# VectorE sums the last rows, and the last attention segment runs without memory work: a two-layer kernel with recurrent-memory attention and a gated MLP

## The chip, the cores and the metric

The kernel runs on one core of one Trainium2 chip. The metric is the device time of one execution in microseconds; for the kernel before, the median of three runs is 1624.42 (1624.3 to 1626.09). One execution was also taken with the hardware profiler; all durations below are from that one.

The core's engines run side by side, each through its own list of instructions: TensorE (PE; its weight loads are PEld), VectorE (DVE), ScalarE (ACT), GpSimd (POOL) and SyncE (SP). SP and POOL issue the DMA transfers. PSUM, into which TensorE writes, has eight banks, numbered 0 to 7 here.

## The reference

```python
h = concatenate([mem, xs])                  # 8 memory rows and the 32 tokens of segment s
q, k, v = h @ Wq, h @ Wk, h @ Wv            # 32 heads of 128
p = softmax(mask(q @ k.T * scale))          # memory seen by all, tokens causal
o = (p @ v) @ Wo
mem = o[:8]; outs.append(o[8:])             # the next segment starts from this memory
...
z = gelu(x @ w_in)                          # gMLP: 512 -> 1376
z2 = layernorm(z[:, 688:])
g = w_sp @ z2 + b_sp                        # 2048 x 2048, over the tokens
return (z[:, :688] * g) @ w_out
...
x = x + A(layernorm(x)); x = x + B(layernorm(x))    # twice, with the same weights
```

`x` is 2048 tokens of 512 values. The attention A goes through 64 segments one after the other, because each needs the memory rows that the one before produced.

## The kernel before, in words

The program is two times `a_block` (attention) and `b_block` (gMLP). In both, the instructions of TensorE, VectorE and ScalarE stay in the order in which the Python code writes them (`ORDERED`, `manual_schedule`); those of POOL and SP are placed by a planner, which may issue a load well ahead of its place in the text, as soon as its buffer is free.

**A segment** (`segment`, L912). For segment s TensorE projects 32 rows (the memory of s and its tokens) in pieces: Q and K of one half of the heads into the tile psQ, then psm, psK, psV (`mm_chunk`, L721). VectorE turns these 128x512 pieces (`qk_T`, L932). Scores psS, their exponentials on ScalarE, and the masked E (`close`, L967) follow. `pv` multiplies by the values into psO; `sums_ahead` and `sums_memory` give the softmax denominators of the memory rows, `sums_tokens` those of the token rows (psT). ScalarE forms the reciprocals as exp(-ln) (Rm for the memory rows, Rt for the token rows, L1089 and L1092). `memory_out` (L1026) writes the memory rows of uT, which the output projection `wo_pairs` (px, L798) and `wo_rest` (L805) need at once: they produce the memory of the next segment, which VectorE folds (`fold`, L894 and L896) and puts into hT (`build_hA`, L903 and L904). The next segment's psQ starts when hT is there. The token rows are written by `tok_out` (L1029) and `last_out` (L1032) later, and their output projection is done one segment later beside the next memory rows; rows that this scheme leaves out (the last eight of each segment, from the oB tiles) are projected in groups of 16 segments by `y_part` into the tile pwB, and summed over four parts in yB (L834, L840). `store_o` (L909, L910) and `store_last` (L811) write the attention's output o_d to HBM.

`fill` puts independent matmuls into a segment: `y_part`'s or, for a later 128-token block, the projections of its last rows (`b_units`). `HALVED` holds one base-36 digit for each segment: how many groups of four 512-column matmuls are issued as two times four of 256 columns.

**Row work between the blocks.** gMLP needs x plus the attention's output, and its layer norm. `y_load` (L222, L224, on POOL) loads 128 rows of x into y_x and of o_d into y_o; the sum is made in halves by VectorE (`y_half`, L238) or, for the last four groups of rows (8 to 11), whole by POOL (`y_add`, L228); `y_stats` makes the statistics in three pieces (two halves L150, one aggregate L152); `y_norm` (L249) writes the normalised rows into ln_xn (two buffers) and stores them to xb_d. Rows are numbered in groups of 128: NB = 16 of them, so NB - 8 to NB - 5 are rows 8 to 11, which the loop's last four segments (s = 60 to 63) work on. Three hooks, `spare1`, `spare2` and `spare3`, place such pieces inside a segment, and `tail` and `loads` at its end. `x_stats` makes the same statistics of the input rows two blocks ahead.

**The end of `a_block`.** After the last segment the remaining statistics and norms of rows 10 and 11 are made, then TensorE runs the closing pass: 64 matmuls into pw (L1245) that project the last segment's tokens. ScalarE copies pw to o_end (L1248) and VectorE adds its halves (L1251). Then `b_block` begins: `project` (L296) makes z for 16 tiles, each into a PSUM tile pz of three banks.

**PSUM banks** in this kernel: accA and accB are banks 0 and 1 (changed round in the second block), att 2 and 3, attO0 4 and 5, attO1 6 and 7. The first pz and every second one take banks 2, 3 and 4, the others 5, 6 and 7. Before, pw lies in accB.

Of the kernel before, what the change touches and what calls it, by code (L numbers as in the profile page):

```python
# [29 lines left out]
LATE_STATS = 14  # L30
HALVED = (
    "0090030030800300605070749020807690007088900050807390307085901070",
    "5080030080200400307790006080729040807490207086900070708190507080",
# [629 lines left out]
def a_block(tc, c, rows, front, MV_in, RS_in, MV_out, RS_out, ahead, wo, S, first):  # L663
# [6 lines left out]
    with ExitStack() as ctx:  # L670
# [137 lines left out]
        yB, stores = {}, []  # L808
# [4 lines left out]
        def wo_last(parts, pwB):  # L813

            for k, units in enumerate(parts):
                for t, (src, h) in enumerate(units):
                    nc.tensor.matmul(pwB[32 * t:32 * t + 32, :], lhsT=src[:, h, :], rhs=wo.head(h).rearrange("p (kt g el) -> p g kt el", kt=4, g=4),  # L817
                                     start=(k == 0), stop=(k == 7), tile_position=(0, 32 * t))
                yield

        def y_part(G, q, last=False):

            groups = [oBs[G][:, :, 32 * g:32 * g + 32] for g in range(4)]
            if last:
                parts = [[(groups[g], 8 * q + k) for g in range(3)] + [(groups[q], 24 + k)] for k in range(8)]
            else:
                parts = [[(groups[g], 8 * q + k) for g in range(4)] for k in range(8)]
            pwB = accA.tile([P, DM], F32, name="pwB")
            for k, _ in enumerate(wo_last(parts, pwB)):
                if k in (0, 3):  # L830
                    yield

            def add(lo, n, src):
                nc.vector.tensor_tensor(out=yB[G][lo:lo + n, :], in0=pwB[src:src + n, :], in1=yB[G][lo:lo + n, :], op=ALU.add)  # L834

            def out():
                n = 96 if last else P
                if q == 0:
                    yB[G] = wk.tile([P, DM], F32, name="yB", bufs=1)
                    nc.vector.tensor_copy(yB[G][0:n, :], pwB[0:n, :])  # L840
                else:
                    add(0, n, 0)
                if last:
                    if q == 2:
                        store_last(G, 0, 64, nc.sync)
                    add(32 * q, 32, 96)
                    if q == 2:
                        store_last(G, 64, 96, nc.sync)
                elif q == 3 and G < NB // 4 - 2:
                    stores.append(lambda: store_last(G, 0, P, nc.sync))  # L850
                elif q == 3:
                    store_last(G, 0, P, nc.sync)

            adds.append(out)
            yield

# [55 lines left out]
        def segment(s, fill, spare1, spare2, spare3, tail, loads):  # L912
# [150 lines left out]
            close(1)  # L1063

# [3 lines left out]
            sums = (psO[1][:, 0, 384:512].rearrange("p (g n) -> p g n", g=2), psO[1][:, :, 320:384])  # L1068
            if not (first and s == 0):
                fill()  # L1070
            sums_ahead(sums[0])
# [3 lines left out]
            memory_out(0, sums[0])  # L1075
            spare1(E)
            pv(1)
            sums_memory(1, sums[1])
            sums_tokens(psT)
            memory_out(1, sums[1])  # L1080
# [7 lines left out]
            Rt = segp.tile([P, 2, 512], F32, name="Rt", tag="Rt", bufs=1)  # L1088
            nc.scalar.activation(out=Rt[:], in_=psT[:], func=ACT.Ln)  # L1089
            for r in range(2):  # L1090
                rt = Rt[:, :, 256 * r:256 * r + 256]
                nc.scalar.activation(out=rt, in_=rt, func=ACT.Exp, scale=-1.0)  # L1092
            run(turns)
            spare2()
# [7 lines left out]
            tok_out(0)  # L1102
            last_out(0)
            fill()
            run(copies)
            tok_out(1)
            last_out(1)
# [23 lines left out]
        seen = pers.tile([P, 1], BF16, name="seen")  # L1131

        def y_load(y, o):
            rows.y_load(y, first, nc.gpsimd, rows.pool.tile([P, DM], F32, name="y_x")[:], o)()
# [8 lines left out]
        for s in range(NSEG):  # L1143
# [12 lines left out]
            def spare1(E):  # L1156
                for y, added in ys:
                    if added:
                        y_stats(y, 0)
                    elif tb < NB - 1:  # L1160
                        if j4 < 3:
                            rows.y_half(y, first, 0, nc.gpsimd)
                    else:
                        nc.gpsimd.tensor_copy(seen[:], E[:, 1, 0, 0:1])
                        rows.y_add(y, first, nc.gpsimd, nc.gpsimd)
                if s == NSEG - 1:
                    y_load(NB - 5, rows.pool.tile([P, DM], F32, name="y_o")[:])
                    rows.y_add(NB - 5, first, nc.gpsimd, nc.gpsimd)
# [4 lines left out]
                if (first or tb + 2 >= LATE_STATS) and j4 == 1 and tb + 2 < NB:  # L1173
                    x_stats(tb + 2, 0)
# [6 lines left out]
            def spare2():  # L1181
                if first and s == 8:
                    c["cast_bsp"] = c["load_bsp"]()
                if first and s == 12:
                    c["cast_bsp"]()
                for y, added in ys:
                    if added:
                        y_stats(y, 1)
                    elif tb < NB - 1:
                        rows.y_half(y, first, int(j4 < 3), nc.gpsimd)  # L1190
                if (first or tb + 2 >= LATE_STATS) and j4 == 1 and tb + 2 < NB:
                    x_stats(tb + 2, 1)

            def spare3():
                for y, added in ys:
                    if added:
                        y_stats(y, 2)
                    elif tb < NB - 1 and j4 == 3:
                        rows.y_half(y, first, 1, nc.gpsimd)
                if (first or tb + 2 >= LATE_STATS) and j4 == 1 and tb + 2 < NB:  # L1200
                    x_stats(tb + 2, 2)
                if s == NSEG - 1:
                    for k in range(3):
                        y_stats(NB - 6, k)

            def tail():
                if j4 == 1 + 2 * (first and tb == 0) and tb + 1 < NB:
                    spread_v(blk_state[tb + 1])
                if tb == NB - 1:
                    if j4 != 2:  # L1210
                        front.load_w(j4)
                    if j4 > 0:
                        front.load_rows(j4 - 1)
                if ys and ys[0][1]:
# [6 lines left out]
            def loads():  # L1221
                if due and s < NSEG - 1 and (not ys or tb == NB - 1):
                    y = due.pop(0)
                    ys.append([y, False])
                    if tb < NB - 1 or j4 == 0:
                        y_load(y, rows.pool.tile([P, DM], F32, name="y_o")[:])
                    elif j4 == 1:
                        nc.vector.memset(rowsB[:, 0, 0:1], 0.0)
                        y_load(y, rowsB[:].rearrange("p a n -> p (a n)").bitcast(F32))
                    else:  # L1230
                        y_load(y, wo.VX[0][:].rearrange("p j r e -> p (j r e)").bitcast(F32))

            segment(s, lambda n=1: [next(more, None) for _ in range(n)], spare1, spare2, spare3, tail, loads)
        assert due == [NB - 5] and ys == [[NB - 6, True]]
# [6 lines left out]
        pw = accB.tile([P, 512], F32, name="pw")  # L1241
        for i in range(H // 2):
            for k in range(4):
                h = 2 * i + k % 2
                nc.tensor.matmul(pw[32 * k:32 * k + 32, :], lhsT=ends[k // 2][:, h, :], rhs=wo.head(h).rearrange("p (kt g el) -> p g kt el", kt=4, g=4),  # L1245
                                 start=(i == 0), stop=(i == H // 2 - 1), tile_position=(0, 32 * k))
# [46 lines left out]
```

## Time and profile before

| what | value |
|---|---|
| median of the runs (lowest, highest) | 1624.42 us (1624.3, 1626.09) |
| the profiled execution: its time, its span | 1624.41 us, 1622.7 us |
| mean granted TensorE clock | 0.996 |
| TensorE, VectorE, ScalarE, GpSimd busy | 97%, 75%, 65%, 18% |
| one undisturbed segment | 10.00 us |
| s = 61, 62 in the first block, 125, 126 in the second | 10.01, 10.48, 10.00, 10.48 us |

The profile gives for each group of instructions its line, engine, operation and tiles, the busy time, the mean duration of one, and how long the engine stood idle just before them with the instruction that ended it. A wait is written as `engine line <- releaser`, with its sum, its number and its longest. A timeline gives the start and the duration of each instruction in order. Segment 61 of the first block begins at 659.55 us, 62 at 669.56 and 63 at 680.04; in the second block, the segments are counted on, so that 64 is its first: 125 begins at 1448.80, 126 at 1458.80 and 127 at 1469.28.

### The profile page before, as it was taken

What the parts mean: (1) busy time and instruction counts of PE and PEld (TensorE: products, weight loads), DVE (VectorE), ACT (ScalarE), POOL (GpSimd) and SP (SyncE); (2) the same over time, 40 slices, a digit from 0 to 9 for tenths busy, and PEclk for the clock granted to TensorE, in tenths of its full rate; (3) what the DMA queues carried; (4) which work ended last, traced back from release to release, by engine and by line L of the source; (5) the groups of instructions that cost most, each with busy time, mean ns of one, the idle gap of its engine ahead of it and who ended that gap; (6) DMA issues with size and microseconds to landing.
All of it is one profiled execution on the core that took longest, in us unless ns stands there. A gap on an engine that the chain in (4) does not pass through costs nothing.

```text
span 1622.7 us, 93662 instructions
## 1 busy us (share of the span) xinstructions
PE 1568.9 (97%) x42251; PEld 992.3 (61%) x42274; DVE 1212.3 (75%) x3181; ACT 1062.4 (65%) x2278; POOL 286.3 (18%) x604
## 2 busy tenths in 40 slices
PE   3899999999999999999999999999999999999999
PEld 1456666666666666666656666666666666665565
DVE  3677777788887887884467777777888788878722
ACT  2577777777777777661047777777777777775400
POOL 5111111111211122320011111111121112214000
PEclk9899999999999999999999999999999999999999
DMA  9322212213322334276962222222233233335696
GB/s 346 110 47 43 43 43 44 46 43 76 82 55 44 76 90 82 88 191 140 208 183 48 44 50 47 46 47 48 62 95 81 47 69 98 92 56 171 141 199 162
DMA packets 264760, 149.47 MB, mean 92 GB/s; under 512 B 198680, under 2 KB 240784, under 8 KB 264360
## 3 DMA queue, kind: packets, MB, share of 16 engines
q1 hardware_dynamic: 251128, 99.66, 28.6%
q0 software_dynamic: 13232, 43.82, 8.4%
q8 instruction: 331, 5.42, 1.4%
q14 instruction: 69, 0.57, 0.1%
HBM read 59.68 MB, written 37.19 MB: 60 GB/s over the span
## 4 chain that ended last, share of the span: by engine, by line
PE 92%; DMA 4%; ACT 1%; DVE 1%; issue 1%; POOL 1%; SPq 0%; POOLq 0%; DVEq 0%
PE psQ L721 13%; PE psK L721 13%; PE psb L721 9%; PE pg L396 9%; PE px L798 8%; PE psV L721 7%; PE psm L721 7%; PE psO L805 6%; PE pz L296 5%; PE psO L1007 3%; PE pwB L817 3%; PE py L439 2%; PE psT L999 2%; PE psS L955 2%; DMA Wk_sb<-in_A_Wk_dram 1%; DMA Wo_high<-in_A_Wo_dram 1%
## 5 line engine op out<-in xcount | busy, mean ns | idle before, releaser
L721 PEld LDWEIGHTS <-hT 128*32 128x32 bf16 x13904 | 365.8, 96 | 286.1 <-DVE hT L904 67.0
L932 DVE STREAM_TRANSPOSE QQ<-rows 128x512 bf16<-128x512 bf16 x256 | 179.3, 701 | 19.6 <-ACT rows L929 12.7
L932 DVE STREAM_TRANSPOSE KA<-rows 128x512 bf16<-128x512 bf16 x256 | 176.3, 689 | 12.6 <-ACT rows L929 11.3
L929 ACT CAST rows<-psQ 128x512 bf16<-128x512 f32 x256 | 142.2, 584 | 20.1 <-PE psQ L721 19.4
L396 PE MATMUL pg<-z,wspT 128*128 128x344 bf16 x1024 | 154.3, 309 | 0.0
L1026 DVE TENSOR_TENSOR uT<-psO,Rm 128x128 bf16<-128x128 f32 x256 | 74.6, 291 | 105.6 <-PE psO L1010 57.1
L1092 ACT ACTIVATE Rt<-Rt 128x512 f32<-128x512 f32 x256 | 147.3, 622 | 4.1
L1029 DVE TENSOR_TENSOR uT<-psO,Rt 128x384 bf16<-128x384 f32 x256 | 140.8, 550 | 11.6 <-ACT Rt L1092 4.5
L964 ACT ACTIVATE S<-psS 128x224 bf16<-128x224 f32 x256 | 91.4, 357 | 82.8 <-PE psS L959 82.8
L721 PE MATMUL psQ<-Wq_sb,hT 128*32 128x512 bf16 x2048 | 135.2, 381 | 8.7 <-ACT Rt L1089 5.1
L798 PEld LDWEIGHTS <-uT 128*32 128x32 bf16 x4608 | 111.0, 96 | 47.8 <-DVE uT L1026 32.5
L798 PE MATMUL px<-Wo,uT 128*32 128x256 bf16 x3840 | 134.8, 274 | 0.6 <-DMA Wo<-in_A_Wo_dram 0.6
L721 PE MATMUL psK<-Wk_sb,hT 128*32 128x256 bf16 (+1 forms) x2796 | 134.7, 322 | 0.0
L721 PE MATMUL psK<-Wv_sb,hT 128*32 128x512 bf16 (+1 forms) x2620 | 134.6, 333 | 0.0
L721 PE MATMUL psm<-Wq_sb,hT 128*32 128x512 bf16 x2048 | 134.4, 379 | 0.1
L721 PE MATMUL psQ<-Wk_sb,hT 128*32 128x512 bf16 x2048 | 134.2, 379 | 0.0
L721 PE MATMUL psV<-Wv_sb,hT 128*32 128x512 bf16 (+1 forms) x2344 | 133.6, 351 | 0.0
L1089 ACT ACTIVATE Rt<-psT 128x1024 f32<-128x1024 f32 x128 | 131.0, 1024 | 3.1
L396 PEld LDWEIGHTS <-wspT 128*128 128x128 bf16 x1024 | 100.2, 98 | 53.2
L805 PE MATMUL psO<-Wo_high,uT 128*32 128x128 bf16 x7168 | 124.3, 220 | 1.9 <-DMA Wo_high<-in_A_Wo_dram 1.9
L888 POOL COPY KX<-old 128x128 bf16<-128x128 bf16 x128 | 68.2, 547 | 305.1 <-PE psS L959 248.8
L1024 ACT ACTIVATE Rm<-psO 128x128 f32<-128x128 f32 x256 | 71.0, 277 | 74.0 <-PE psO L981 74.0
(194 smaller groups left out, 2895.0 us busy)
## 6 DMA issues: line engine op xcount, KB each, us to landing
o_d<-o_sb SPq DMA_DIRECT2D x126, 64.0 KB
vb_d<-front SPq DMA_DIRECT2D x30, 256.0 KB
VX<-vb_d SPq DMA_DIRECT2D x120, 64.0 KB
ln_x<-xd SPq DMA_DIRECT2D x26, 256.0 KB
y_o<-o_d POOLq DMA_DIRECT2D x22, 256.0 KB, 3.6
xd<-y_o POOLq DMA_DIRECT2D x22, 256.0 KB, 3.0
Wq_sb<-in_A_Wq_dram POOLq DMA_DIRECT2D x8, 512.0 KB, 10.1
Wk_sb<-in_A_Wk_dram POOLq DMA_DIRECT2D x8, 512.0 KB, 11.1
```

Of the source, the lines that this page charges most:

```text
L296: nc.tensor.matmul(pz[:, c0:c1], lhsT=xnT[:, kt, :], rhs=w_in_sb[:, kt, c0:c1], start=(kt == 0), stop=(kt == KT - 1))
L396: nc.tensor.matmul(pg[t][:, k, 0:344], lhsT=wsp[t][:, st, :], rhs=z(st, 344 * k, 344 * k + 344), start=(st == 0), stop=(st == NT - 1))
L721: mms.append(nc.tensor.matmul(ps[32 * cg:32 * cg + 32, n * k:n * k + n], lhsT=lhs(kt, cg), rhs=r[:, m * k:m * k + m], start=(kt == 0), sto ...
L798: nc.tensor.matmul(px[at:at + 32, 0:256], lhsT=lhs[:, h, :], rhs=wo_rhs(h, slice(k + 2, None, -2) if h % 2 else slice(k, None, 2)), start= ...
L805: nc.tensor.matmul(pw[32 * cg:32 * cg + 32, :], lhsT=lhs[:, h, :], rhs=wo_rhs(h, cg), start=False, stop=(h == H - 1), tile_position=(0, 32 ...
L929: return r, mms, nc.scalar.copy(r[:], ps)
L932: nc.vector.transpose(out=QQ[:, j % 2, :, 0:32] if j < 2 else KA[:, j % 2], in_=r[:])
L964: return nc.scalar.activation(out=S[:, r], in_=psS[:, r, 0:224], func=ACT.Exp, scale=scale)
L1026: nc.vector.tensor_tensor(out=hview(uT_cur[:], r, 24, 32), in0=oview(r, 0, 8), in1=rm.rearrange("p g (n q) -> p g n q", q=8), op=ALU.mult)
L1029: nc.vector.tensor_tensor(out=hview(uT_nxt[:], r, 0, 24), in0=oview(r, 8, 32), in1=rview(r, 0, 24), op=ALU.mult)
L1089: nc.scalar.activation(out=Rt[:], in_=psT[:], func=ACT.Ln)
L1092: nc.scalar.activation(out=rt, in_=rt, func=ACT.Exp, scale=-1.0)
```

## The change

Three things are changed in `a_block`, and one table.

The row work gets one more hook, `spare0`, which stands behind the second masked E (`close(1)`), ahead of `pv`. A segment's pieces of row work are spread over four hooks, as a rule one piece in each: the first half sum or first half statistic in `spare0`, the second in `spare1`, the aggregate in `spare3`. `x_stats` is spread over two segments (j4 = 1 and 2). 

The last rows, 8 to 11, are no longer summed by POOL but by VectorE, in the places that the new table `FINAL` names: its keys are (segment within the last block, hook), its entries (row minus 8, piece, index). Row 8 is summed in s = 61, row 9 in s = 62 and 63, row 10 at the end of 63; row 11 behind the loop.

In the last segment the memory rows' work is left out (nothing follows that would need a memory: the rows that it would have written are overwritten by `store_last`), the token factors are formed where it stood, and `tok_out` and `last_out` come ahead of the fold. The closing pass's tile pw is taken from att in place of accB, and its matmuls start with the upper heads. The last group's three parts of pwB are summed in PSUM in one tile, ScalarE copies the extra rows into yB, and one VectorE add and one store close it.

`HALVED` has other digits; most are larger.

```diff
+FINAL = {(1, 0): ((0, "sum", 0),), (1, 1): ((0, "sum", 1),),
+         (2, 0): ((0, "stats", 0),), (2, 1): ((0, "stats", 1),), (2, 2): ((1, "sum", 0),), (2, 3): ((0, "stats", 2),),
+         (3, 0): ((1, "sum", 1),), (3, 1): ((1, "stats", 0),), (3, 2): ((1, "stats", 1),),
+         (3, 3): ((1, "stats", 2), (2, "sum", 0), (2, "sum", 1))}
 HALVED = (
-    "0090030030800300605070749020807690007088900050807390307085901070",
-    "5080030080200400307790006080729040807490207086900070708190507080",
+    "0386908690878078906080729040708070807080708070708190507070807084",
+    "6392907690869080030807070807080709060708290407080707080708080649",
 )
...
-            pwB = accA.tile([P, DM], F32, name="pwB")
+            if not last or q == 0:
+                held["pwB"] = accA.tile([P, DM], F32, name="pwB")
+            pwB = held["pwB"]
...
+                if last:
+                    nc.scalar.copy(yB[G][32 * q:32 * q + 32, :], pwB[96:128, :])
+                    if q == 2:
+                        add(0, 96, 0)
+                        store_last(G, 0, 96, nc.sync)
+                    return
...
             close(1)
+            spare0()
...
+            ends_here = s + 1 == NSEG
...
             pv(0)
-            memory_out(0, sums[0])
+            if not ends_here:
+                memory_out(0, sums[0])
             spare1(E)
             pv(1)
...
-            memory_out(1, sums[1])
+            if ends_here:
+                spare2()
+                token_factors((1, 0))
+            else:
+                memory_out(1, sums[1])
             run(copies)
             px = accB.tile([P, 512], F32, name="px")
             wo_pairs(px, uT_cur)
...
+            if ends_here:
+                fill()
+                for r in (1, 0):
+                    tok_out(r)
+                    last_out(r)
+            else:
+                token_factors((0, 1))
+                run(turns)
+                spare2()
...
+            def final(slot):
+                for y, op, k in FINAL.get((j4, slot), ()) if tb == NB - 1 else ():
+                    (y_stats if op == "stats" else y_sum)(NB - 8 + y, k)
+
+            def spare0():
+                final(0)
                 for y, added in ys:
                     if added:
                         y_stats(y, 0)
                     else:
-                        nc.gpsimd.tensor_copy(seen[:], E[:, 1, 0, 0:1])
-                        rows.y_add(y, first, nc.gpsimd, nc.gpsimd)
+                        y_sum(y, 0)
...
+                if (first or tb + 2 >= LATE_STATS) and j4 in (1, 2) and tb + 2 < NB:
+                    x_stats(tb + 2, j4 - 1)
...
-        assert due == [NB - 5] and ys == [[NB - 6, True]]
+        assert due == [NB - 5] and not ys
+        y_norm(NB - 7, nc.sync)
+        for k in range(3):
+            y_stats(NB - 6, k)
+        for k in range(2):
+            y_sum(NB - 5, k)
         for k in range(3):
             y_stats(NB - 5, k)
         run(copies)
         for y in (NB - 6, NB - 5):
             y_norm(y, nc.sync)
         ends = (uT[NSEG % 2], oBs[NB // 4 - 1][:, :, 96:128])
-        pw = accB.tile([P, 512], F32, name="pw")
-        for i in range(H // 2):
+        pw = att.tile([P, 2, 512], F32, name="pw")[:, 0, :]
+        for n in range(H // 2):
+            i = (n + H // 4) % (H // 2)
```

## The prediction

> **What bounds the kernel now.** I read the page first (busy shares, slices, the chain), then the list of waits, then the timelines of the places that the diff touches: the segments s = 61 and s = 63 of the first attention block (from 659.55 and 680.04 us), and their twins 125 and 127 in the second (from 1448.80 and 1469.28). Times with a plus are counted from the start of a segment, which is its first psQ matmul.
>
> ```profile
> span 1622.7 us, 93662 instructions
> PE 1568.9 (97%) x42251; PEld 992.3 (61%) x42274; DVE 1212.3 (75%) x3181; ACT 1062.4 (65%) x2278; POOL 286.3 (18%) x604
> PE   3899999999999999999999999999999999999999
> PE 92%; DMA 4%; ACT 1%; DVE 1%; issue 1%; POOL 1%; SPq 0%; POOLq 0%; DVEq 0%
> PEld L721 <- DVE hT L904: 67.0, 243, 0.9
> PEld L721 <- issue: 10.4, 28, 1.2
> POOL y_o L224 <- DMA o_d<-yB: 17.6, 3, 9.2
> ```
>
> TensorE is busy 97% of the span, and a clean segment takes 10.00 us of it. So VectorE work is worth something only where TensorE stands waiting for it, and new VectorE work costs only where it makes TensorE wait. The waits for hT are mostly weight loads that come early and cost nothing. The "issue" line is TensorE out of instructions. POOL's last line is the one to remember: the load of a summed row waits for the store of yB.
>
> **Moved row work (spare0, FINAL).** VectorE runs strictly in program order, so an operand that comes late holds all that is written behind it.
> ```profile
> 662.18 0.56 SPq L811 DMA_DIRECT2D o_d<-yB  x1
> 665.66 0.54 POOL L224 DMA_DIRECT2D y_o<-o_d  x1 [9.25 <-DMA o_d<-yB]
> 665.70 0.38 DVE L967 TENSOR_TENSOR E<-S,maskN 128x448 bf16<-128x448 bf16 x1
> 666.57 0.29 DVE L1026 TENSOR_TENSOR uT<-psO,Rm 128x128 bf16<-128x128 f32 x1 [0.49 <-PE psO L1010]
> 669.08 1.16 POOL L228 TENSOR_TENSOR y_o<-y_o,y_x 128x512 f32<-128x512 f32 x1 [1.87 <-DMA y_o<-o_d]
> ```
> This is s = 61. VectorE is free from 666.08 to 666.57, and the new spare0 goes there. A half sum takes 0.41 us (L238: 13.2 us over 32), 0.34 from issue to issue, a half statistic 0.42: one piece fits into the 0.49 us if its row is there. In the ordinary segments I took each y_o landing from the transfers: it is later than the slot by enough to push uT (normally at +7.02) in six segments, 37, 53, 99, 101, 115 and 117, by 0.20, 0.07, 0.36, 0.15, 0.82 and 0.50 us (landing + 0.09 to start + 0.34 - 7.02). TensorE's output pass px waits for uT, with nothing between: +2.1 us. Before, the same sum stood behind uT.
>
> At s = 61 the late row is row 8. Its load can't be issued before the yB store has landed (665.66 = +6.11; in segment 125 at +6.81), and lands at +9.38 and +10.61. FINAL's entry (1, 0) puts its first half sum ahead of uT: uT comes at 9.38 + 0.09 + 0.37 = +9.84 instead of +7.02, and at about +11.0: +2.8 and +4.0 us, +6.8 together. Queued behind are uT, px, the fold and hT, so all of it reaches TensorE. In the profile of before the same lateness only held POOL's adds, each of 1.16 us, which nobody waited for; that these adds and POOL's `seen` copies (0.20 us) go is worth nothing, since POOL is busy 18%. Its loads and stores stay as many. SP's two yB stores at the end become one (0.7 us less on a queue that is not late). If a gap of POOL's L224 moved by 1 us, the term would be 4.8 to 8.8.
>
> **Statistics of x spread over two segments.** Three pieces in one segment push hT late: TensorE's psQ starts 0.2 to 0.3 us late in segments 36, 38, 50, 69, 104, 114 and 118, 0.6 in 54. Spread, they fit: -1.3. At s = 62 the two yB operations of the segment before (0.68 + 0.69) stand ahead of the first transposes and TensorE waits 0.48 us; ScalarE's copy takes their place: -0.48 per block, -1.0. ScalarE is 65% busy and its 0.6 us copy stands where nobody waits, so it is costed at nothing; were that cover gone, at 0.6 per block.
>
> **HALVED.** A unit of a digit turns four matmuls into eight and costs about 2 ns (a segment without takes 10.00, with nine units 10.02); the digits go from 404 to 531 in all: +0.3 us. But they also shift where TensorE's instruction pages end. All stalls of L721 for "issue" inside segments sit at instruction 194 or 195 of a page of 256, in ten places (0.2 to 1.2 us), 4.9 us in all, where a page was run in about 3.2 us. The new digits make two segments and their eight units five pages, so that ends fall at fixed places with a shortest page of 3.4 to 3.6 us: I take -2.2 (bounds -4.9, all stalls gone, and +1.5, five more of 0.3 us).
> Were the Trainium skill ("Runtime: NRT & Kernel Launch", Instruction fetch mechanics) right that the end of a 16 KiB block of 256 instructions is mostly hidden, this term would be 0 and the time 2.2 us longer; the ten stalls speak for a cost that is not hidden.
>
> **The end of the block.**
> ```profile
> 692.43 0.39 PE L1245 MATMUL pw<-Wo,uT 128*32 128x512 bf16 x2 [1.16 <-DVE uT L1029]
> 694.59 0.55 DVE L249 TENSOR_SCALAR ln_xn<-rowsB,MV,RS 128x512 bf16<-128x512 f32 x1
> 696.19 6.12 PE L296 MATMUL pz<-front 128*128 128x512 bf16 x29
> 696.51 0.57 ACT L1248 COPY o_end<-pw 128x512 f32<-128x512 f32 x1
> 698.15 0.55 DVE L249 TENSOR_SCALAR ln_xn<-y_o,MV,RS 128x512 bf16<-128x512 f32 x1 [1.68 <-DMA xb_d<-ln_xn]
> 698.73 1.40 DVE L1251 TENSOR_TENSOR o_end<-pw,o_end 32x512 f32<-32x512 f32 x2
> ```
> Before, in s = 63, TensorE waits 0.86 us for the first transposes (1.80 in segment 127), 1.16 for uT ahead of the closing pass pw (L1245), then runs pw 3.8 us and the first projection pz at +16.15 (+17.09). Without memory work and with the token factors early, pw can start at about +9.9, when the fill ends, and pz at about +13.5: -2.65 and -3.6, -6.25 in all.
>
> What is late next is pw's bank. Before, pw lay in accB's bank, which pz does not use; so its readers, ScalarE's o_end copy and VectorE's two adds, could end at 700.13, 3.9 us after pz began. Now pw takes the att tile: banks 2 and 3. The first pz takes banks 2 to 4. So TensorE waits until the copy and both adds are done, and they stand last in VectorE's order. I followed that order with the rows above: last_out(0) ends at +10.4; the fold, o_sb, the aggregate of row 9 and both sums of row 10 to +12.1; ScalarE's yB copy, then VectorE's add on 96 rows +12.6 to +13.3 (0.69); y_norm of row 9 to +13.8; statistics of row 10 to +14.6, two sums and the statistics of row 11 to +16.2; y_norm of row 10 beside; then y_norm of row 11. This takes the ln_xn buffer of row 9, whose store lands 3.0 us after its norm (694.59 + 0.55 to 698.15), so at +16.9 to +17.4; then the adds, 1.40, to +18.86. pz begins at +18.9 instead of +13.5: +5.4. In segment 127 that store took 4.2 us (1485.33 to 1489.51); between 3.0 and 4.2 I take 3.6: +6.0. Together +11.4; at least 7.0 if the norms' stores are quick (the adds then end at about +17), at most 14 if row 11 is also late by 1.3 us in each.
>
> **Clock.** The profile shows what a long idle does.
> ```profile
> 22.20:25.80 3.60, 0.02 (x4) 0.09 (x1) 0.00 (x0) 0.72 (x3) 1.12 (x3) 1.00 1.04 395
> 25.80:29.20 3.40, 3.29 (x32) 1.39 (x35) 2.26 (x5) 1.13 (x3) 1.53 (x3) 0.50 1.01 405
> 42.85:46.26 3.41, 1.47 (x42) 1.01 (x43) 2.30 (x8) 0.86 (x3) 0.88 (x3) 1.00 1.01 344
> 46.26:49.60 3.34, 0.61 (x6) 0.13 (x6) 0.00 (x0) 0.00 (x0) 0.00 (x0) 0.50 1.03 350
> ```
> After the length of the stretch stands TensorE's busy time; the last three numbers are the granted clock, the DMA share and GB/s. After 3.6 us with none the clock was 0.50 for 3.4 us, and also after 3.41 us with 1.47 busy; a full stretch at half speed costs 1.7 us. The idle of 5.4 and 6.0 us at pz: 1.7 each. That of 2.85 and 4.05 us at s = 61: 0.85 to 1.7; I take 0.8 and 1.2 with the chance that a stretch holds too much work. Sum +5.4 (bounds 0 and 6.8).
> The Trainium skill ("TensorE: Matmul & The Clock Gate", Part 1) asks for a whole idle window of 3413 ns. By that rule the 2.85 us costs nothing and the 4.05 us seldom does: about 2.0 us less than my sum, 1637.2. The row from 42.85 with 1.47 us of work in it was followed by half clock, which speaks against it.
>
> **Sum.** The profiled execution took 1624.41 (span 1622.7 and 1.7 around it), as the median of the runs, 1624.42. Gains: -1.3 - 1.0 + 0.3 - 2.2 - 6.25 = -10.4. Losses: 2.1 + 6.8 + 11.4 = 20.3. Clock 5.4. Together +15.3: 1639.7; I say 1639, since each loss is nearer to its upper end than to its lower.
>
> **The rivals.**
> A, not slower: pz does not wait for pw. If pz took its first banks elsewhere, or the adds ended by +13.5 (that decides), 11.4 and 3.4 of clock go: 1639.7 - 14.8 = 1624.9, from 1621 to 1627. For it: last_out ends almost 3 us earlier than before (692.95 + 0.28 = +13.2). Against: banks 2 to 4 are pz's in this kernel, and nothing in the diff moves o_end ahead of the norms. Chance 0.10.
> B: s = 61 does not stall. If row 8 lands by +6.5, 6.8 and 2.0 of clock go: 1630.9. Against: its load was issued at +6.11 and +6.81, and lands 3.3 to 3.8 us later; the store's place is unchanged. Chance 0.12.
> C: the change does what it says and neither wait shows: 1624.4 - 10.4 + 2.1 = 1616.1. Chance 0.08.
> D, my forecast: both waits. Chance 0.70, within it 1630 (quick stores, no half clock: -4.4 - 5.4) to 1646 (the upper bounds of the losses and the clock: +2.0 + 2.6 + 1.4).
>
> **How the numbers follow.** About 0.2% (3.25 us) is what a measurement of this kernel can tell from no change. C is faster, and 0.03 of A: 0.11. The rest of A is the same: 0.07. B and D are slower: 0.82. The range must leave out no more than 0.2: without A and C, 0.18, it runs from 1628, which takes in most of B (down to 1626.5 with quick stores), to 1646.
>
> **What would show it.** In s = 61 and 125 VectorE's half sum of row 8 waits for the y_o transfer, and uT comes near +9.8 and +11.0, with TensorE idle 2.8 and 4.0 us in front of px; the first pz matmul of each block waits 5 to 6 us for VectorE's o_end, at +18.9 and +19.5; half clock in the stretches behind; fewer and shorter stalls for issue. The prediction is wrong if pz starts by +15, if uT in s = 61 stays near +7, or if L721's stalls for issue grow.

## The result and the profile after

The changed kernel takes 1642.89 us (median of six runs, 1640.08 to 1646.95) against 1624.36 (six runs, 1622.82 to 1626.09): slower by 1.16%, with a 95% interval of the ratio of 1.0103 to 1.0129. The profiled execution took 1642.10, its span is 1640.4. The forecast was 1639 with a range of 1628 to 1646.

The lines of the page and of the list of waits that answer to those shown of before:

```profile
span 1640.4 us, 94604 instructions
PE 1571.5 (96%) x42719; PEld 1007.9 (61%) x42742; DVE 1211.5 (74%) x3183; ACT 1063.5 (65%) x2276; POOL 278.9 (17%) x590
PE   4899999999999999989999999999999999998999
PE 91%; DMA 5%; DVE 2%; ACT 2%; issue 1%; POOL 0%; DVEq 0%; POOLq 0%
PEld L725 <- DVE hT L910: 65.4, 250, 0.9
PEld L725 <- issue: 11.1, 25, 1.5
POOL y_o L228 <- DMA o_d<-yB: 17.1, 3, 9.4
```

TensorE's busy time is nearly the same, 1571.5 us against 1568.9, and the span is 17.7 longer: the loss is TensorE waiting, or working at half clock. Two of the 40 slices of TensorE's row have an 8 that had a 9, the 18th (697 to 738 us) and the 37th (1476 to 1517): these are the starts of the two gMLPs.

Here is s = 61 of the first block (it starts at 658.73 now), VectorE's, POOL's and TensorE's timelines in turn:

```profile
664.87 0.38 DVE L973 TENSOR_TENSOR E<-S,maskN 128x448 bf16<-128x448 bf16 x1
669.24 0.43 DVE L242 TENSOR_TENSOR y_o<-y_o,y_x 128x256 f32<-128x256 f32 x1 [3.98 <-DMA y_o<-o_d]
669.58 0.28 DVE L1032 TENSOR_TENSOR uT<-psO,Rm 128x128 bf16<-128x128 f32 x1
...
664.95 0.54 POOL L228 DMA_DIRECT2D y_o<-o_d  x1 [9.36 <-DMA o_d<-yB]
...
669.92 1.89 PE L802 MATMUL px<-Wo,uT 128*32 128x256 bf16 x30 [3.76 <-DVE uT L1032]
```

VectorE stands 3.98 us in front of the half sum of row 8, whose load could be issued only at 664.95; uT is behind it, and TensorE's px behind uT. The end of the block (s = 63 starts at 683.85):

```profile
697.25 0.53 DVE L253 TENSOR_SCALAR ln_xn<-rowsB,MV,RS 128x512 bf16<-128x512 f32 x1
700.97 0.58 ACT L1287 COPY o_end<-pw 128x512 f32<-128x512 f32 x1
701.77 0.55 DVE L253 TENSOR_SCALAR ln_xn<-y_o,MV,RS 128x512 bf16<-128x512 f32 x1 [0.96 <-DMA xb_d<-ln_xn]
702.34 1.40 DVE L1290 TENSOR_TENSOR o_end<-pw,o_end 32x512 f32<-32x512 f32 x2
704.00 2.29 PE L300 MATMUL pz<-front 128*128 128x512 bf16 x5 [6.69 <-DVE o_end L1290]
```

pw ended at about 697.3, and the first pz began 6.69 us later, when the two adds that read pw had ended at 703.74. In the second block it waits 7.43 us. There the profile names a store of ln_xn as what came last; the adds ended 0.58 us before pz, and the experiments on the bank below decide.

Where the 17.7 us are, from the starts of the segments in the two profiles:

| place | before | after | difference | forecast |
|---|---|---|---|---|
| to the end of segment 11 | 164.98 | 163.55 | -1.4 | 0 |
| segments 12 to 60 and 65 to 124 | 1097.04 | 1097.67 | +0.6 | -1.1 |
| segments 61 and 125 | 20.00 | 29.01 | +9.0 | +8.8 |
| segments 62 and 126 | 20.96 | 20.02 | -0.9 | -1.0 |
| segments 63 and 127, to the first pz | 33.24 | 41.05 | +7.8 | +5.2 |
| from the first pz to the end of each gMLP | 276.46 | 279.03 | +2.6 | +3.4 |

The first row holds the loading of the weights at the start; in the profiles of all the kernels here it lies between 163.55 and 167.14.

### The profile page after: what moved, and what is told of

It is laid out like the page before. It is cut to its first block, busy times and chain, and to the rows that moved or that the text cites. A ratio compares the mean times of both kernels' runs of the same rounds, so it can differ in the third digit from the quotient of the medians.

```text
span 1640.4 us, 94604 instructions
## 1 busy us (share of the span) xinstructions
PE 1571.5 (96%) x42719; PEld 1007.9 (61%) x42742; DVE 1211.5 (74%) x3183; ACT 1063.5 (65%) x2276; POOL 278.9 (17%) x590
## 4 chain that ended last, share of the span: by engine, by line
PE 91%; DMA 5%; DVE 2%; ACT 2%; issue 1%; POOL 0%; DVEq 0%; POOLq 0%
PE psQ L725 13%; PE psK L725 13%; PE psb L725 9%; PE pg L400 9%; PE px L802 8%; PE psm L725 7%; PE psV L725 6%; PE psO L809 6%; PE pz L300 5%; PE psO L1013 3%; PE pwB L821 3%; PE py L443 2%; PE psT L1005 2%; PE psS L961 1%; DMA Wk_sb<-in_A_Wk_dram 1%; DMA Wo_high<-in_A_Wo_dram 1%
## 5 line engine op out<-in xcount | busy, mean ns | idle before, releaser
L725 PEld LDWEIGHTS <-hT 128*32 128x32 bf16 x14412 | 378.7, 96 | 277.3 <-DVE hT L910 65.4
L802 PEld LDWEIGHTS <-uT 128*32 128x32 bf16 x4608 | 112.1, 97 | 54.4 <-DVE uT L1032 39.0
L725 PE MATMUL psQ<-Wq_sb,hT 128*32 128x512 bf16 x2048 | 134.1, 381 | 7.7 <-ACT Rt L1080 5.1
L725 PE MATMUL psK<-Wv_sb,hT 128*32 128x512 bf16 (+1 forms) x2852 | 134.3, 319 | 1.0 <-issue 1.0
L725 PE MATMUL psK<-Wk_sb,hT 128*32 128x256 bf16 (+1 forms) x2952 | 134.0, 314 | 0.0
L725 PE MATMUL psQ<-Wk_sb,hT 128*32 128x512 bf16 x2048 | 133.7, 379 | 0.3 <-issue 0.3
L725 PE MATMUL psm<-Wq_sb,hT 128*32 128x512 bf16 x2048 | 133.5, 379 | 0.0
L725 PE MATMUL psV<-Wv_sb,hT 128*32 128x512 bf16 (+1 forms) x2464 | 133.3, 342 | 0.0
L809 PEld LDWEIGHTS <-uT 128*32 128x32 bf16 x7168 | 115.7, 98 | 3.7 <-issue 3.1
```

Of the source, the lines that this page charges most:

```text
L725: mms.append(nc.tensor.matmul(ps[32 * cg:32 * cg + 32, n * k:n * k + n], lhsT=lhs(kt, cg), rhs=r[:, m * k:m * k + m], start=(kt == 0), sto ...
L802: nc.tensor.matmul(px[at:at + 32, 0:256], lhsT=lhs[:, h, :], rhs=wo_rhs(h, slice(k + 2, None, -2) if h % 2 else slice(k, None, 2)), start= ...
L809: nc.tensor.matmul(pw[32 * cg:32 * cg + 32, :], lhsT=lhs[:, h, :], rhs=wo_rhs(h, cg), start=False, stop=(h == H - 1), tile_position=(0, 32 ...
```

## The experiments

Each is compared with runs of the kernel before on its own chip; a "changed kernel" is the one above. The kernel before has medians of 1622.55 to 1626.74 there, so a difference of 2 us between runs that were measured at different times means little by itself, and the ratios count. Each kernel has one profile, of one execution.

**Each wait alone.** First the sums of row 8, put where a late row holds nothing that the segment needs:

```diff
-FINAL = {(1, 0): ((0, "sum", 0),), (1, 1): ((0, "sum", 1),),
+FINAL = {(1, 3): ((0, "sum", 0), (0, "sum", 1)),
```

> The changed kernel with one edit: both half sums of row 8 stand in the last hook of s = 61 (behind hT), not ahead of uT. Theory (two separate waits): the stall in s = 61 and 125 with its half clock goes, 5.1 + 3.9 us by the changed kernel's segments, so 1642.9 - 9.0 = 1634; VectorE then reaches the first transposes of s = 62 up to 0.75 us later, which may give back 0.2 per block. Rival 1 (VectorE's row work as a whole is too much, wherever it stands): the time stays above 1640. Rival 2 (the stall is only moved: the late row holds VectorE in the later hook just as long): s = 62 gets longer by 2 us or more and the time is 1638 to 1641.

Measured: 1634.09 us (before 1623.78; ratio 1.0063, 1.0048 to 1.0078). VectorE in s = 61, and the two segments 61 and 125 as stretches (length, TensorE busy, and so on):

```profile
667.22 0.25 DVE L910 STREAM_TRANSPOSE hT<-memT 128x64 bf16<-128x64 bf16 x1
667.57 0.74 DVE L242 TENSOR_TENSOR y_o<-y_o,y_x 128x256 f32<-128x256 f32 x2
```
```profile
657.21:667.21 10.00, 10.00 (x310) 6.00 (x309) 8.00 (x22) 7.09 (x16) 2.19 (x5) 1.00 0.31 88
1450.82:1460.83 10.01, 10.01 (x332) 6.65 (x332) 8.01 (x22) 7.08 (x16) 2.17 (x5) 1.00 0.32 90
```

The same two operations behind hT cost nothing: TensorE is busy in 10.00 of 10.00 us, and s = 62 stays at 10.02. The stall is the place of the sum in VectorE's order, not the work. Both rivals fall.

Then the bank. pw goes back to accB; px lies there before it, so its readers come earlier, and the exponentials of the token factors go behind ScalarE's copy of px (the first call makes the logarithm alone):

```diff
-                token_factors((1, 0))
+                token_factors(())
...
+                token_factors((1, 0), False)
                 fill()
+                fold(px, cross, t1, beside)
                 for r in (1, 0):
                     tok_out(r)
                     last_out(r)
...
-        pw = att.tile([P, 2, 512], F32, name="pw")[:, 0, :]
+        pw = accB.tile([P, 512], F32, name="pw")
```

> The changed kernel with the closing pass's tile back in accB's bank; so that accB is free in time, the fold of the last segment is made before the last rows of uT (ScalarE's copy beside it ahead of the two exponentials). Theory (the first pz waits for the readers of pw because they share bank 2): pz begins at +13.5 to +14.2 in place of +20.15 and +20.90, and the half clock behind it goes (1.0 to 1.9 each): 1642.9 - 6.4 - 7.1 - 3 = 1626.4. Rival (pz is late for another reason, its rows or weights, or VectorE's backlog holds the first tiles anyway): pz still begins at +17 or later and the time is above 1636.

Measured: 1634.43 us (ratio 1.0075, 1.0049 to 1.0101). The wait was there because of the bank: pz now begins at +13.61 and +13.62, while the adds still end at +19.50 and +21.17. But only 8.5 of the 16.5 us came back. In the second block, from the first pz to the end took 143.04 us, against 137.91 in the changed kernel and 136.33 before. TensorE's waits among the pz matmuls of the second block, from its timeline:

```profile
1495.47 4.81 PE L300 MATMUL pz<-front 128*128 128x512 bf16 x24 [1.20 <-ACT z L301]
1507.65 9.47 PE L300 MATMUL pz<-front 128*128 128x512 bf16 x48 [2.72 <-DMA front<-xb_d]
1523.92 9.47 PE L300 MATMUL pz<-front 128*128 128x512 bf16 x48 [2.16 <-DMA front<-xb_d]
```

A tile has 12 of these matmuls. The third tile waits for the GELU of the first, which stands behind the factor of row 11, the copy of pw and a table load on ScalarE; the seventh and the thirteenth wait for their rows, which come back transposed from xb_d. None of this showed before, when pz began at +16.15 and +17.09: the profile has no wait among its pz matmuls. A start at +13.6 runs into what was ready only later.

**Both edits.**

> Both edits together. Theory: the two waits are independent and add: 1642.9 - 9.0 - 16.5 = 1617.4, faster than before by 7 us, since what is left are the gains of the change less the late rows. Rival (the end of the block gives part back, because the later row 8 pushes VectorE's chain behind it): 1620 to 1624.

Measured: 1626.29 us (before 1623.78; ratio 1.0011, 0.9999 to 1.0022), not 1617.4, and above the rival's range too. The two waits add, 8.8 and 7.8 us. Of the 8.9 us that are missing, 6.8 are again behind pz: 140.68 and 142.56 us to the ends of the two blocks (before 140.12 and 136.33).

```profile
1499.75 11.10 PE L300 MATMUL pz<-front 128*128 128x512 bf16 x48 [2.29 <-DMA front<-xb_d]
```

The seventh tile of the second block waits 2.29 us for its rows, and the 48 matmuls from there take 11.10 us in place of 9.47, since the granted clock is 0.50 for 3.4 us from 1499.67 on.

**The chain behind row 11.** In the run with both edits, VectorE stood 2.82 us in front of row 11's norm for ln_xn's buffer, with SP's stores and, behind them, the transposes. Here that norm has a buffer of its own:

```diff
-        for y in (NB - 6, NB - 5):
-            y_norm(y, nc.sync)
+        y_norm(NB - 6, nc.sync)
+        rows.y_norm(NB - 5, MV_out[:, NB - 5, 0:1], RS_out[:, NB - 5:NB - 4], nc.sync, rowsB[:, 0, :])
```

> Both edits (row 8 later, accB), and the norm of row 11 written to a buffer that is free, so that it does not wait 2.8 us for the store of row 9's. Theory (what held the end of the block in the run with both edits is the chain behind row 11's norm: o_end, SP's stores and then the transposes of xb_d, for which the eighth and later tiles wait 2.3 and 0.5 us in the second block): these waits go, 1626.3 - 2.8 = 1623.5. Rival (the transposes are late because transfers are slow there, not because they are issued late): the waits stay and so does the time, 1625.5 to 1627.

Measured: 1623.16 us (before 1622.55; ratio 1.0004, 0.9992 to 1.0015). The number is the theory's, but the ratio of the run with both edits, 1.0011 (0.9999 to 1.0022), can't be told from this one; what shows the chain is the profile, in which the wait of the seventh tile is gone. In the second block one wait for rows is left, that of the thirteenth:

```profile
1483.43 4.81 PE L300 MATMUL pz<-front 128*128 128x512 bf16 x24 [1.21 <-ACT z L301]
1507.99 9.47 PE L300 MATMUL pz<-front 128*128 128x512 bf16 x47 [1.16 <-DMA front<-xb_d]
```

With that the last segment without memory work can be priced. From the start of s = 63 to the end of the gMLP, the profile of this run has 155.88 and 152.78 us, that of before 156.27 and 153.42: 1.0 us for both blocks, where pz begins 2.5 and 3.5 us earlier. Such stretches differ by more than that where only digits of HALVED differ: in the kernel before with the new digits alone (below) they take 155.42 and 152.49. And this profile is of the fastest of its ten runs. So the gain is some 1 us at most, and it isn't shown that there is one.

**The bank in the kernel before.** One line, nothing else:

```diff
-        pw = accB.tile([P, 512], F32, name="pw")
+        pw = att.tile([P, 2, 512], F32, name="pw")[:, 0, :]
```

> The kernel before with one edit: pw is taken from att instead of accB. Theory (the first pz waits for pw's readers only because of the bank): o_end's adds still end at +20.1 and +22.2, and pz starts behind them, 4.2 and 5.2 us later than before, with half clock behind each idle (1.0 to 1.9): 1624.2 + 9.4 + 2.8 = 1636. Rival (the delay is absorbed in the gMLP, whose first tiles wait for rows anyway): under 1630.

Measured: 1638.39 us (before 1622.55; ratio 1.0095, 1.0080 to 1.0110). pz begins at +21.19 and +21.51, 5.0 and 4.4 us later, 0.10 us behind the last add in each block. This one line alone makes the kernel 1% slower, and the rival falls.

**The clock.** The changed kernel, with matmuls that nobody uses in TensorE's idle time:

```diff
             px = accB.tile([P, 512], F32, name="px")
+            if s == NSEG - 3:
+                busy(px[:], 9)
             wo_pairs(px, uT_cur)
...
+        busy(attO[1].tile([P, 2, 512], F32, name="psO")[:, 0, :], 26)
         o_sb = segp.tile([P, DM], F32, name="o_end", tag="Rt", bufs=1)
```

> The changed kernel, with matmuls that compute nothing that is used put into TensorE's idle times: 9 of 512 columns (1.9 us) ahead of px in s = 61 and 125, and 26 (5.6 us) between pw and the first pz, into a bank that is free. No wait is removed. Theory (half clock follows an idle stretch): the granted clock stays 1.00 behind both waits, and 1.3 + 1.7 in s = 61 and 125 and 1.0 + 1.6 behind pz are saved: 1642.9 - 5.6 = 1637.3. Rival (what is lost beyond the waits is not the clock, or half clock does not follow idle): 1642 to 1644, with the clock at 0.50 in the same places.

Measured: 1640.83 us (before 1622.55; ratio 1.0112, 1.0095 to 1.0129). Against the kernel before that is 18.3 us more, where the changed kernel has 18.5: as a whole nothing was gained, where the theory had 5.6. The granted clock (the last number but two) is in these stretches. The changed kernel first: the waiting stretch and the one behind it in segments 61 and 125, and the start of pz in the first block. Then this run: the gap, now with work in it, and the stretch behind it in s = 61, and the start of pz:

```profile
665.80:669.20 3.40, 0.35 (x10) 0.02 (x2) 0.00 (x0) 0.59 (x2) 1.29 (x4) 1.00 0.49 159
669.20:672.60 3.40, 2.68 (x68) 2.19 (x72) 1.57 (x6) 0.49 (x2) 1.07 (x2) 0.50 0.21 77
1464.50:1467.90 3.40, 1.24 (x46) 0.89 (x44) 1.16 (x4) 0.59 (x2) 1.38 (x5) 1.00 0.51 154
1467.90:1471.30 3.40, 3.40 (x88) 2.52 (x84) 1.47 (x7) 2.40 (x4) 1.01 (x2) 0.50 0.48 158
703.35:706.75 3.40, 2.75 (x7) 1.02 (x8) 0.39 (x1) 0.00 (x0) 2.09 (x4) 0.50 0.74 221
```
```profile
666.20:669.60 3.40, 2.26 (x18) 0.84 (x13) 0.00 (x0) 0.59 (x2) 1.55 (x4) 1.00 0.52 158
669.60:673.00 3.40, 2.52 (x108) 2.09 (x108) 2.22 (x9) 1.28 (x2) 1.07 (x2) 1.00 0.21 78
703.20:706.60 3.40, 3.40 (x17) 1.66 (x18) 0.00 (x0) 0.75 (x1) 1.44 (x3) 1.00 0.87 294
```

The clock theory holds in all four places: with work in the gap the clock stays at 1.00, in the second block too (1468.80 to 1472.20 and 1504.45 to 1507.85). Segments 61 and 125 take 13.97 and 12.33 us in place of 15.11 and 13.90, the stretches from pz to the end 139.18 and 136.42 in place of 141.12 and 137.91: 6.1 us in sum. But segments 65 to 124 of the second block took 6.7 us more. In that profile TensorE waits there for late rows (1.5, 1.1 and 0.5 us in 99, 115 and 103) and in many places for instructions, at the ends of the instruction pages of 256, which the inserted matmuls had moved. What the run gained at the waits it lost there. That the inserted matmuls caused it is not shown: other kernels here have such losses in single profiles too.

**The digits of HALVED**, three times. The run with both edits, with the old digits:

```diff
-    "0386908690878078906080729040708070807080708070708190507070807084",
-    "6392907690869080030807070807080709060708290407080707080708080649",
+    "0090030030800300605070749020807690007088900050807390307085901070",
+    "5080030080200400307790006080729040807490207086900070708190507080",
```

> As with both edits, but with the digits of HALVED of the kernel before. By the forecast's term the new digits are worth 2.2 - 0.3 us, so this run would be 1.9 slower than the one with both edits. Theory now (the stalls for instructions come from transfers that hold up the fetch, and the digits only move them about): within 1 us of it, to either side.

Measured: 1631.40 us (before 1623.78; ratio 1.0054, 1.0038 to 1.0071), 5.1 more than with the new ones on the same chip. The kernel before, with the new digits alone (the same lines the other way round):

> The kernel before with the new digits of HALVED alone. The forecast's term: 1624.2 - 2.2 + 0.3 = 1622.3. Theory after the first runs (a digit's worth depends on where page ends fall beside transfers, so digits of one layout are worth little in another): 1623 to 1627, to either side.

Measured: 1622.22 us (before 1622.55; ratio 0.9996, 0.9987 to 1.0006). The interval is -2.1 to +1.0 us: it takes in nothing as well as the forecast's -1.9. For the third see below. Neither side of the first expectation was right. In the profile with both edits and the old digits px waits 6.5 us for a late uT (segments 35, 37, 49, 53, 55, 89, 99, 103 and 119), with the new ones 0.6; the one with the old digits is of the slowest of its four runs, 3.7 us above their median.

**Late rows ahead of uT.** That made me try the run with row 11 mended with the ordinary half sums behind uT: the first in spare1 or spare2, the second in spare3.

```diff
             def spare0():
...
-                    else:
-                        y_sum(y, 0)
...
             def spare1(E):
...
                     elif j4 < 3:
-                        y_sum(y, 1)
+                        y_sum(y, 0)
...
             def spare2():
...
                     if not added and j4 == 3:
-                        y_sum(y, 1)
+                        y_sum(y, 0)
...
             def spare3():
...
+                    else:
+                        y_sum(y, 1)
```

> The run with row 11's norm mended (row 8 later, accB), and the ordinary half sums taken out of the hook ahead of uT: the first goes behind the memory rows of uT or, in every fourth segment, into the third hook, the second behind hT. Theory (a late y_o load ahead of uT costs TensorE what it is late, 0.5 us in that run's profile but 4.4 and 7.2 us in the profiles of two others of these kernels, so it also makes the runs differ): no wait of px for uT in any segment, 1618 to 1621, and the runs lie within 4 us. Rival (the runs differ for another reason, such as the instruction fetch): 1622 to 1624 as before, with the spread of 9 us left.

Measured: 1627.51 us (before 1625.17; ratio 1.0016, 1.0006 to 1.0027), and the runs lie from 1623.79 to 1633.01. The time is above both ranges, but the rival's mechanism holds: the late rows are not what makes the runs differ. In this profile the waits for uT are 0.8 us in sum, none behind a late row, but segments 97 to 124 take 3.4 us more than before, 1.1 of it in one segment with a stall for instructions, and the thirteenth tile of pz waits 2.35.

The same with ScalarE's copy of pw ahead of row 11's factor (`run(copies)` issues the factors; row 11's norm, which needs its factor, goes behind the copy with it):

```diff
         for k in range(3):
             y_stats(NB - 6, k)
+        run(copies)
...
         for k in range(3):
             y_stats(NB - 5, k)
-        run(copies)
...
         nc.scalar.copy(o_sb[:], pw[:])
+        run(copies)
```

> The same, with ScalarE's copy of pw ahead of the factor of row 11. Theory (the third pz waits 1.2 to 1.3 us for the first GELU, which stands behind that factor, the copy and the loading of ScalarE's table): that wait falls by 0.6 in each block, 1 us less than the run beside it. Rival (the tiles behind it wait for the transposes of xb_d in any case, so that a shorter wait there is given back): the same time within 0.5 us.

Measured: 1629.58 us (ratio 1.0023, 1.0011 to 1.0034). The wait for the GELU falls to 0.72 and 0.59, as the theory has it, and more than that is given back: from the first pz to the end the blocks take 144.22 and 144.00 us, against 141.81 and 140.46 in the run beside. Tiles 7 and 13 wait for their rows, and the last 48 matmuls run at half clock in part (10.76 in place of 9.47):

```profile
1490.31 4.81 PE L300 MATMUL pz<-front 128*128 128x512 bf16 x24 [0.59 <-ACT z L301]
1501.96 9.47 PE L300 MATMUL pz<-front 128*128 128x512 bf16 x48 [2.20 <-DMA front<-xb_d]
1519.03 10.76 PE L300 MATMUL pz<-front 128*128 128x512 bf16 x48 [2.81 <-DMA front<-xb_d]
```

**What is worth keeping.** Two parts of the change in the kernel before: `x_stats` in `spare2` of j4 = 1 and in `spare2` and `spare3` of j4 = 2, and the last group of yB summed in one PSUM tile, with ScalarE's copies (the hunks of `wo_last`, `y_part` and `out` as in the change); first with the old digits, then with the new.

```diff
             def spare2():
...
-                if (first or tb + 2 >= LATE_STATS) and j4 == 1 and tb + 2 < NB:
-                    x_stats(tb + 2, 1)
+                if (first or tb + 2 >= LATE_STATS) and j4 in (1, 2) and tb + 2 < NB:
+                    x_stats(tb + 2, j4 - 1)
```

> The kernel before with two parts of the change alone: the statistics of x spread over two segments, and the last group of yB summed in PSUM with ScalarE's copies. The end of the block, the place of the row sums and the digits of HALVED stay. Theory (these parts work as the forecast has them, and are worth what their waits were): TensorE's waits for hT fall from 2.2 us to under 0.4, those for KA at the start of s = 62 go (0.5 in each block), 1.3 to 3 us in all: 0.1 to 0.2% faster than before. Rival (the instructions' new places bring as many stalls for instructions): the same time, within 0.1%.

> The same with the new digits of HALVED. Theory: the digits add nothing that can be told (within 1.5 us of the run beside it), as in the kernel before with the digits alone. Rival (the digits belong to the rest of the change and are worth 5 us only with it, as between the two runs with both edits): this run is also 2 us or more faster than the run beside it.

Measured: 1620.85 us (before 1626.74; ratio 0.9965, 0.9952 to 0.9978) with the old digits, faster than the kernel before by 0.35%, and 1625.29 (ratio 0.9989, 0.9980 to 0.9998) with the new. The waits for hT did not go as I expected: the row sums still stand in the same hook, and psQ now starts 0.18 to 0.28 us late in thirteen segments, 2.6 us in sum. The gain is where the two yB operations stood, ahead of the first transposes of s = 63: TensorE waited 0.68 and 1.62 us for these (KA) in segments 63 and 127 before, and doesn't now. In this profile pz begins at +15.03 and +15.19, 1.1 and 1.9 earlier, and from there to the end takes 140.38 and 136.44 us, as before (140.12 and 136.33). So some 3 us come from these parts. The rest of this profile's 5.9 us is 1.2 in the loading at the start and some 2 in the ordinary segments, where the stalls for instructions at page ends are 2.7 us against 4.9 before; such stalls differ by as much without a change (next section, HALVED). With the new digits they are 8.4, and the time is 4.4 us more: neither the theory nor the rival.

## Why the prediction was right, step by step

**Row 8 at s = 61.** Right in place and mechanism, and in size as a sum: 3.8 and 2.2 us of waiting where +2.8 and +4.0 stood, 6.0 against 6.8 in sum. The two blocks changed places because the load landed at +10.4 and +8.8 this time. Moving the sums alone took 8.8 us off.

**pw's bank.** Right in place and mechanism: +20.15 and +20.90 where +18.9 and +19.5 stood. The chain came out as written down to row 9's norm (+13.4). What was too short is the store of that norm: 4.0 and 4.4 us to its release (697.25 + 0.53 to 701.77 in the first block), where 3.0 and 3.6 had been taken. pz then began 0.26 and 0.58 us behind the last add, where nothing had been taken.

**Clock.** 5.4 forecast. Measured from the two profiles: segment 61 lost 5.11 us with 3.83 of waiting, so 1.3; segment 125 lost 3.90 with 2.2, so 1.7; behind pz 1.0 and 1.6: 5.5. The single terms were 0.8, 1.2, 1.7 and 1.7, so the closeness of the sum is partly luck. The Trainium skill ("TensorE: Matmul & The Clock Gate", Part 1) asks for an idle window of 3413 ns. In segment 125 TensorE waited 2.2 us in all, and the stretch with 1.24 us of work was followed by half clock. So here the row decided, and the forecast by the row was nearer. (The prediction's 1637.2 by the other is a slip: 1639.7 - 2.0 is 1637.7.) The price is not a sure one: in the run with pw back in accB, TensorE waited 2.06 us at the same place of segment 125, the clock stayed at 1.00, and the segment took 12.14 us, not 13.90.

**hT and s = 62.** The starts of psQ were late by 2.2 us in sum before and by 0.1 after (forecast 1.3 less); s = 62 and 126 went to 10.01 as forecast.

**Late rows.** 2.1 forecast. In the profile a late row pushes uT in segments 35, 37, 39 and 53, by 1.2, 0.2, 0.6 and 0.3 us: 2.3 in sum, but only 37 and 53 are among the six segments that were named, so the sum was right by luck. The six were taken from one execution's landings; in other kernels of this case the same hook cost from 0.4 to 6.5 us. It is a term with a wide range, and I gave it none.

**HALVED.** This term was wrong: -1.9 forecast. Counted as in the forecast (weight loads that wait for instructions at a page's end, segments 12 to 126), the stalls were 4.9 us in ten places before and are 4.3 in six now, the longest 0.9 before and 1.5 now. Over the whole list, L721's stalls for issue went from 10.4 to 11.1 us (L725 now): they grew, which the forecast had named as a sign of being wrong. The ordinary segments, with the late rows in them, have +0.6 where -1.1 was forecast. The step that failed is to take the stalls of one profile as those of the program. In the first block, the kernel before and the run with the bank's one line alone have the same matmuls, and their profiles have 3.6 and 0.5 us of such stalls. I had counted only when a page is used up, not when its fetch can begin. The largest stall, 1.5 us in segment 120, had a fetch (a packet of 16,384 bytes) that began, by a count of the instructions, 4.0 us after the page before was entered, while three transfers of rows of 256 KB each were under way. That transfers hold the fetch up is what this window suggests; no run here takes the transfers away, so it isn't shown. The Trainium skill ("Runtime: NRT & Kernel Launch", Instruction fetch mechanics) calls the end of a block mostly hidden. With 1.1 to 8.4 us of stalls at these places in the profiles it is not wholly hidden in this kernel.

**The intended gain.** The term of -6.25 us assumed that pz at +13.5 is worth its 2.65 and 3.6. It had to be paired with the bank wait, which hid the error. With the wait gone, the gain was 1.0 in one profile, less than these stretches differ where only digits differ. So rival A's 1624.9 (measured 1634.43) and rival C's 1616.1 (1626.29 with both edits) were too low by 9.5 and 10.2 us, and B's 1630.9 (1634.09) by 3.2. I asked what is late next once, for pw's bank, and did not ask it again of the tiles behind the first: their GELU, and the rows that come back transposed.

**The sum.** That 1639 came so near 1642.9 is luck in part: the end of the block was 2.6 us more than forecast and the ordinary segments 1.7, against 1.4 less at the start and 0.8 less behind pz. The two waits and their clock, which decide the sign and most of the size, were shown one by one.

**What stays open.** Why the executions of the kernels with an early pz differ by 7 to 9 us (before: 3 to 7), and why the digits are worth 5 us in one arrangement, nothing in another and -4.4 in a third.

## What to carry to other kernels

On an engine that runs in program order, a piece of work is priced by when its operand lands and by what stands behind it, not by its length: the same 0.74 us cost 9 us ahead of uT with its clock, and nothing behind hT. A new PSUM tile is priced by the next tile in its banks and by where its last reader stands on its own engine. And a stage that can start earlier gains only up to the next thing that was just in time before; ask for it again after every wait that is taken away.

## What was not expected of the hardware

In these 14 profiles the granted clock changes only on a grid of 3.41 us (in the changed kernel at 669.18, 672.59 and 699.90, for example). Counted on this grid, and from 60 us on, every stretch in which TensorE had worked for 1.35 us or less was followed by half clock, and none with 1.54 us or more was. So a wait of some 2 us costs clock or not by where it falls: in segment 125 of the run with pw back in accB the grid cuts it in two, with 2.63 and 2.14 us of work in the two stretches.

And 6.7 us were lost in a later stage of the run with matmuls put into idle time, nearly half of it to late rows, the rest to stalls for instructions. Work that delays nothing where it stands can't be counted as free from the profile of another program; but one profile doesn't show that this work was the cause.
